# Accumulating DMAs for a spectral sum, and a sixth seven-product down projection, in a two-layer convolution and SwiGLU kernel

## The chip, the cores and the metric

The kernel runs on one core of a Trainium2 chip. The metric is device time in microseconds (us), less is better. TensorE is called PE here (its weight loads PEld), VectorE DVE, ScalarE ACT, GpSimd POOL and SyncE SP, as in the profile. SP, ACT and POOL can each start DMA transfers; "SPq" is SP's DMA queue.

## The reference

Two equal layers work on `x`, 2048 tokens by D = 512 (bf16). A layer is a gated long convolution followed by a SwiGLU block of width F = 1792; both have residuals and layer norms without gain:

```
def layer(x):
    kv = causal_conv4(k, shift_k) * v            # 4 taps on each channel
    y  = irfft(rfft(kv, 2S) * rfft(ssm_k, 2S))[:S] + kv * ssm_D
    x  = x + layernorm(x) * y
    z  = layernorm(x)
    return x + (silu(z @ w_gate) * (z @ w_up)) @ w_down
```

The convolution's result `y` doesn't depend on `x`: it is the same in both layers and computed once.

## The kernel before, in words

**The long convolution.** The sequence is cut into four chunks of 512 tokens. Each chunk of `kv` is turned into a spectrum `X[i]` and each chunk of the filter into a spectrum `G[j]` by matmuls with a DFT matrix. The output chunk k is the inverse transform of `Z[k]`, the sum of the products `X[i]*G[j]` with i+j = k. A spectrum tile is 128 partitions x 4 x 2 x 512 bf16 values, 8 KB in each partition, 1 MB in all; the axis of 2 holds the real and the imaginary part. There are ten products. `product(i, j)` makes one by four DVE operations: two multiplications of 4096 elements (L765, into `t1` and `t2`) and two combinations of 2048 (L769). The first product of a sum is combined right into `Z`; each of the six others into `t1`, and a fifth operation of 4096 elements adds `t1` to `Z` (L773). The inverse begins with `m <- Z` on DVE (L653) for Z[1] to Z[3].

**The SwiGLU blocks.** A unit (layer, c, h) is half h of chunk c in one layer, 256 tokens; there are 16. Gate and up projections go through L423 (and L1171), ACT takes them out of PSUM (L1197, L1198, L1258, L1262), DVE multiplies them (L1204, L1267). Where that was done with tokens on partitions, an SP DMA transposes the result (L1206: `sg <- hr`). Most units do the down projection by 28 matmuls of 512 columns (L1287); ACT copies the two sums out (`dn`, L1332 or L1335) and DVE adds them to `x` (L1339). Five units, those in `STRASSEN`, go through `seven()`: 49 matmuls of 256 columns (L1097) that make seven block products in place of eight. These need sums of activations (`cb`, three DVE operations for each group of tiles, L1076, L1078, L1080), sums of weights made once (`weight_sums`, L1061), and an end of its own (`add_seven`: ACT copies `mt`, L1109, and five DVE operations, L1114 to L1121). The groups hold 4, 4, 4 and 2 tiles.

**Layer norms.** The statistics of two rows of 128 tokens are made on DVE (`ln_stats`: L926 and L927, twice) or on ACT (`ln_stats_act`, L941 to L954), and POOL raises them to the power -1/2 (`rstd`, L912). `ST2` lists the halves whose second layer norm has its statistics on ACT.

**The order of the work.** The program first records all operations with their engine, reads and writes (`add`). The list `ORDER` gives each operation a number, and the operations are issued in this order on their engines; semaphores keep what depends on each other. Buffers come from rings with a fixed count of places (`s8` has 11 of 8 KB; `z` has 3, `jk` one); an operation that takes a place waits for the last reader of what was there.

Of the kernel before, what the change touches and what calls it, by code (L numbers as in the profile page):

```python
# [9 lines left out]
P = 128  # L10
F32 = mybir.dt.float32
# [3 lines left out]
ALU = mybir.AluOpType  # L15
# [6 lines left out]
ST2 = lambda l, c, h: (l, c, h) in {(0, 0, 0), (0, 2, 1), (1, 2, 1)}  # L22
K_ACT = lambda b: b in {2, 3}
PW = 0.7
# [6 lines left out]
STRASSEN={(1,2,1):4,(0,3,0):4,(0,3,1):4,(1,3,0):4,(1,3,1):2}  # L31
# [96 lines left out]
R = 4  # L128
# [222 lines left out]
def kernel(  # L351
# [14 lines left out]
    nc = tc.nc  # L366
# [46 lines left out]
    add = plan.add  # L413
# [326 lines left out]
    def product(i, j, slots=range(4), conv=True):  # L740
# [31 lines left out]
        if not first:  # L772
            dve(8 * D, lambda: nc.vector.tensor_add(out=z.t[:], in0=z.t[:], in1=t1.t[:]), [t1], [z], conv=conv)  # L773
# [832 lines left out]
```

## Time and profile before

| | |
|---|---|
| median of 3 runs | 338.73 us (338.35 to 338.96) |
| span of the profiled execution, first to last instruction | 337.1 us |
| median less that span | 1.63 us |
| granted TensorE clock | 1.000 |
| busy: PE, DVE, ACT, POOL | 332.4, 314.3, 269.4, 36.1 us |
| traffic | 31.08 MB, mean 92 GB/s |

The profiled execution has no time of its own beside its span; the 1.63 us are what the median has over it. The busy time of an engine counts an instruction from its start to its end, and matmuls are pipelined: a row's mean ns of one matmul is longer than the step from one to the next. Steps are therefore read from the chain of waits, where a run of matmuls is one piece with its count.

### The profile page before, as it was taken

Reading aid. Unit: us, or ns where it says so; the run is one execution under the profiler, and the core shown is the slowest. Engines: PE = TensorE matmul, PEld = TensorE weight load, DVE = VectorE, ACT = ScalarE, POOL = GpSimd, SP = SyncE. Lnnn points to the kernel's source line nnn. Section 1 sums busy time; section 2 is a strip of 40 time slices with the busy share of each in tenths; the row PEclk is TensorE's granted clock in tenths of the full one; section 3 lists DMA queues with packets and bytes.
Section 4 is the critical chain, followed back from the end, with each engine's and each line's share of the span. In section 5 each row is a group of like instructions: output and inputs, shape, how many; then the busy total and the mean of one; then the engine's idle time right before and its main releaser. Section 6 shows DMA issues by size and latency. Waiting matters only on the chain.

```text
span 337.1 us, 6249 instructions
## 1 busy us (share of the span) xinstructions
PE 332.4 (99%) x2300; PEld 208.0 (62%) x2300; DVE 314.3 (93%) x566; ACT 269.4 (80%) x550; POOL 36.1 (11%) x48
## 2 busy tenths in 40 slices
PE   9999999999999999999999999999999999999996
PEld 7665865645445564644545474654445787878994
DVE  7799999999999999999999999997898998986995
ACT  6999999999966684989999794989765748476862
POOL 4010100031210100022110200021000000000000
PEclk9999999999999999999999999999999999999999
DMA  7999403632354446253314433320415320203001
GB/s 278 331 281 387 65 3 77 140 93 34 78 94 86 95 88 146 72 80 74 69 33 83 104 81 102 81 53 10 84 33 95 65 65 16 42 8 64 2 33 62
DMA packets 75817, 31.08 MB, mean 92 GB/s; under 512 B 67589, under 2 KB 73610, under 8 KB 75786
## 3 DMA queue, kind: packets, MB, share of 16 engines
q1 hardware_dynamic: 75632, 30.61, 38.3%
q8 instruction: 18, 0.29, 0.4%
q14 instruction: 13, 0.11, 0.1%
q10 hardware_dynamic: 154, 0.07, 0.1%
HBM read 12.33 MB, written 2.10 MB: 43 GB/s over the span
## 4 chain that ended last, share of the span: by engine, by line
PE 85%; DVE 10%; ACT 2%; issue 1%; POOL 0%; POOLq 0%
PE pf L423 48%; PE pd L1287 19%; PE ps L1097 7%; PE ps L423 6%; PE pf L1171 4%; DVE t L755 1%; PE wm L1572 1%; DVE Z L759 1%; DVE bst L926 1%; DVE t L769 1%; ACT jk L950 1%; DVE Z L773 1%; DVE t L765 1%; DVE m L896 1%; DVE z L976 1%
## 5 line engine op out<-in xcount | busy, mean ns | idle before, releaser
L423 PEld LDWEIGHTS <-zT 128*128 128x128 bf16 x496 | 48.5, 98 | 55.1 <-issue 0.2
L423 PE MATMUL pf<-wu_sb,zT 128*128 128x512 bf16 x248 | 61.5, 379 | 0.0
L423 PE MATMUL pf<-wg_sb,zT 128*128 128x512 bf16 x248 | 61.4, 379 | 0.0
L423 PE MATMUL pf<-zT,wg_sb 128*128 128x256 bf16 x400 | 50.7, 273 | 0.3 <-DVE zT L1037 0.3
L1197 ACT ACTIVATE sg<-pf 128x512 bf16<-128x512 f32 x62 | 37.4, 615 | 14.9 <-PE pf L423 10.7
L1287 PE MATMUL pd<-wd_sb,sg 128*128 128x512 bf16 x200 | 48.9, 379 | 0.0
L1198 ACT CAST hr<-pf 128x512 bf16<-128x512 f32 x62 | 36.3, 599 | 12.7 <-PE pf L423 10.9
L423 PEld LDWEIGHTS <-wg_sb 128*128 128x128 bf16 x400 | 38.6, 98 | 8.3 <-issue 0.7
L765 DVE TENSOR_TENSOR t<-X,G 128x4096 bf16<-128x4096 bf16 x18 | 41.0, 2287 | 0.1
L1258 ACT ACTIVATE sg<-pf 128x512 bf16<-128x512 f32 x50 | 29.6, 603 | 7.7 <-PE pf L423 6.3
L423 PE MATMUL pf<-zT,wu_sb 128*128 128x256 bf16 x272 | 34.9, 273 | 0.1
L912 POOL TENSOR_TENSOR rstd<-mv,nhalf 128x2 f32<-128x2 f32 x20 | 18.3, 919 | 147.8 <-DVE mv L927 147.8
L1287 PEld LDWEIGHTS <-sg 128*128 128x128 bf16 x200 | 19.6, 98 | 21.4
L423 PEld LDWEIGHTS <-wu_sb 128*128 128x128 bf16 x272 | 26.5, 98 | 6.6 <-issue 0.4
L1287 PE MATMUL pd<-wd_sb,ht 128*128 128x512 bf16 (+1 forms) x126 | 29.6, 369 | 0.0
L912 POOL TENSOR_TENSOR rstd<-ve,nhalf 128x2 f32<-128x2 f32 x12 | 13.8, 1150 | 119.6 <-ACT ve L954 119.6
L926 DVE BATCH_NORM_STATS2 bst<-xc 128x6 f32<-128x512 bf16 x40 | 26.3, 685 | 0.3
L1262 ACT CAST ht<-pf 128x512 bf16<-128x512 f32 x34 | 20.2, 599 | 1.6 <-PE pf L423 1.5
L1287 PEld LDWEIGHTS <-ht 128*128 128x128 bf16 x126 | 12.3, 98 | 13.4 <-DVE ht L1267 0.4
L532 ACT ACTIVATE X<-ps 128x512 bf16<-128x512 f32 x32 | 18.6, 606 | 2.3 <-PE ps L423 1.6
L1267 DVE TENSOR_TENSOR ht<-ht,sg 128x1024 bf16<-128x1024 bf16 (+1 forms) x33 | 18.3, 556 | 0.7 <-ACT sg L1258 0.4
L1204 DVE TENSOR_TENSOR hr<-hr,sg 128x1024 bf16<-128x1024 bf16 x25 | 17.1, 683 | 1.3 <-ACT sg L1197 0.9
(157 smaller groups left out, 590.9 us busy)
## 6 DMA issues: line engine op xcount, KB each, us to landing
hn<-in_A_ssm_k_dram SPq DMA_DIRECT2D x4, 512.0 KB, 4.0
vt<-in_A_v_dram SPq DMA_DIRECT2D x4, 512.0 KB, 6.0
xc<-in_A_q_dram SPq DMA_DIRECT2D x4, 512.0 KB, 5.3
out_dram<-xc SPq DMA_DIRECT2D x15, 128.0 KB, 1.9
wg_sb<-in_B_w_gate_dram SPq DMA_DIRECT2D x1, 1792.0 KB
wu_sb<-in_B_w_up_dram SPq DMA_DIRECT2D x1, 1792.0 KB, 7.6
wd_sb<-in_B_w_down_dram SPq DMA_DIRECT2D x1, 1280.0 KB, 11.5
sg<-hr SPq DMA_TRANSPOSE x62, 2.4
```

Of the source, the lines that this page charges most:

```text
L423: nc.tensor.matmul(o, lhsT=lhsT, rhs=rhs, start=(n == 0), stop=(n == len(terms) - 1))
L532: add("ACT", act(D), lambda: nc.scalar.activation(out=view(), in_=ps.t[:], func=ACT.Copy, scale=scale), r=[ps], w=[(buf, keys)], conv=conv)
L765: dve(8 * D, lambda t=t, part=part: nc.vector.tensor_mul(out=t.t[:], in0=x.t[:, :, part:part + 1, :].to_broadcast((P, R, 2, D)), in1=g.t[: ...
L912: add("POOL", cost, lambda: nc.gpsimd.tensor_tensor(out=rstd.t[:], in0=var(), in1=nhalf.t[:].to_broadcast((P, n)), op=ALU.pow), r=reads + ...
L926: add("DVE", 0.6, lambda st=st, i=i: nc.vector.bn_stats(out=st.t[:, 0:6], in_=xs[c].t[:, i, :]), r=[(xs[c], (i,))], w=[st])
L1097: nc.tensor.matmul(bank.t[:, half_ * C:(half_ + 1) * C], lhsT=lhsT(i), rhs=rhs(i), start=(first and i == 0 and half_ == 0), stop=(last and ...
L1197: add("ACT", act(D), lambda ps=ps, dst=dst, o=o, which=which: nc.scalar.activation(out=rows(dst, o), in_=ps.t[:], func=ACT.Silu) if which ...
L1198: out=rows(dst, o), in_=ps.t[:], func=ACT.Silu) if which == "g" else nc.scalar.copy(out=rows(dst, o), in_=ps.t[:]),
L1258: add("ACT", act(D), lambda ps=ps, o=o, sg=sg: nc.scalar.activation(out=sg.t[:, o:o + 2, :], in_=ps.t[:], func=ACT.Silu), r=[ps], w=[(sg, ...
L1262: add("ACT", act(D), lambda ps=ps, o=o, ht=ht: nc.scalar.copy(out=ht.t[:, o:o + 2, :], in_=ps.t[:]), r=[ps], w=[(ht, (o // 2,))], due=(uni ...
L1267: dve(n * W, lambda sg=sg, ht=ht: nc.vector.tensor_mul(out=ht.t[:], in0=ht.t[:], in1=sg.t[:]), [sg], [ht], due=(unit, k / pairs, 0.0, "h"))
L1287: nc.tensor.matmul((pds[o] if not cs.start else pds[HP]).t[:, cs], lhsT=ht.tiles(q, o), rhs=wt["d"].t[:, ft, cs], start=(ft == std0 and no ...
```

## The change

1. With `Z_DMA` true for every pair, the L773 addition is replaced by a DMA from POOL with `accum_op=ALU.add`, from `t1` to `Z`, both in SBUF. It is 1 MB each time, for the products (1,0), (0,2), (2,0), (2,1), (0,3) and (3,0). It stands at L778 of the kernel after.
2. Unit (1,2,0) joins `STRASSEN`, so six units go through `seven()`.
3. Unit (1,2,1) leaves `ST2`: the statistics of its second layer norm go from ACT to DVE.
4. The ring `jk` gets a second place, and `fq`, used at the start, moves into ring `z`.
5. A new `ORDER` list.

Lines of the kernel after stand 5 further on up to the rings and 7 further on behind `product` (L912 is L919, L1097 is L1104, L1287 is L1294, L1339 is L1346).

```
-ST2 = lambda l, c, h: (l, c, h) in {(0, 0, 0), (0, 2, 1), (1, 2, 1)}
+ST2 = lambda l, c, h: (l, c, h) in {(0, 0, 0), (0, 2, 1)}
+Z_DMA = lambda i, j: True
-STRASSEN={(1,2,1):4,(0,3,0):4,(0,3,1):4,(1,3,0):4,(1,3,1):2}
+STRASSEN={(1,2,0):4,(1,2,1):4,(0,3,0):4,(0,3,1):4,(1,3,0):4,(1,3,1):2}
-    plan = Plan({..., "n": 2, "jk": 1, ...
+    plan = Plan({..., "n": 2, "jk": 2, ...
-    m4, fq = whole("m4", [P, R], F32), whole("fq", [P, P], F32)
+    m4, fq = whole("m4", [P, R], F32), new("z", "fq", [P, P], F32)
...
-        if not first:
+        if not first and Z_DMA(i, j):
+            add("POOL", 1.3, lambda: nc.gpsimd.dma_start(out=z.t[:], in_=t1.t[:], accum_op=ALU.add, max_dma_last_dim=4096), r=[t1], w=[z], lat=7.0, conv=conv)
+        elif not first:
             dve(8 * D, lambda: nc.vector.tensor_add(out=z.t[:], in0=z.t[:], in1=t1.t[:]), [t1], [z], conv=conv)
```

**Where the additions stood.** DVE's order before, at the last product of the sum for output chunk 2 (`Z_1614` is Z[2], `t1_1857` this product, `m_2029` the first step of its inverse transform):

```order
L769 TENSOR_TENSOR t1_1857<-t1_1857,t2_1792 128x4x512
L1267 TENSOR_TENSOR ht_1970<-ht_1970,sg_1993 128x512 [waits Activation_49]
L773 TENSOR_TENSOR Z_1614<-Z_1614,t1_1857 128x4096 [waits DVE_49]
L653 TENSOR_TENSOR m_2029<-Z_1614 128x2048 [waits DVE_49]
L946 SCALAR_TENSOR_TENSOR nm_2034<-sm_2026,mv_1570 128x2 [waits Activation_49]
```

The inverse follows right behind the addition. DVE's order after, at the same product (`Z_1570` is Z[2], `t1_1820` the product), from its last combination on. `DMASW2` is the transfer's semaphore.

```order
L774 TENSOR_TENSOR t1_1820<-t1_1820,t2_1822 128x4x512
L1068 TENSOR_TENSOR wsb_1918<-wd_sb_391 128x1792
L1211 TENSOR_TENSOR hr_1807<-hr_1807,sg_1814 128x1024 [waits DMAHW5_49,DMAHW4_49,Activation_49]
L934 BN_AGGR mv_1923<-bst_85 128x2 [waits DVE_49]
L983 TENSOR_SCALAR n_1925<-xc_1789,nm_1796,rstd_1868 128x512 [waits Pool_49]
L983 TENSOR_SCALAR n_1925<-xc_1789,nm_1796,rstd_1868 128x512
L1211 TENSOR_TENSOR hr_1902<-hr_1902,sg_1909 128x1024 [waits Activation_49]
L983 TENSOR_SCALAR n_1998<-xc_837,nm_1876,rstd_1900 128x512 [waits Pool_49]
L983 TENSOR_SCALAR n_1998<-xc_837,nm_1876,rstd_1900 128x512
```

The list goes on without a gap:

```order
L1005 TENSOR_TENSOR n_1998<-n_1998,Yk_1325 128x1024 [waits DVE_49]
L1006 TENSOR_TENSOR xc_837<-xc_837,n_1998 128x1024 [waits DVE_49]
L933 BN_STATS bst_85<-xc_837 128x6 [waits DVE_49]
L934 BN_AGGR mv_2004<-bst_85 128x2 [waits DVE_49]
L933 BN_STATS bst_85<-xc_837 128x6
L934 BN_AGGR mv_2004<-bst_85 128x2 [waits DVE_49]
L1274 TENSOR_TENSOR ht_1937<-ht_1937,sg_1981 128x1024 [waits DMAHW2_49,DMAHW1_49,Activation_49]
L933 BN_STATS bst_85<-xc_1789 128x6
L934 BN_AGGR mv_1923<-bst_85 128x2 [waits DVE_49]
L969 SCALAR_TENSOR_TENSOR nmr_2014<-mv_2004,rstd_2012 128x2 [waits Pool_49]
L1274 TENSOR_TENSOR ht_1985<-ht_1985,sg_1996 128x512 [waits Activation_49]
L658 TENSOR_TENSOR m_2056<-Z_1570 128x2048 [waits DMASW2_49]
```

Nineteen other instructions now stand between the last combination and the inverse, and the inverse waits for the transfer.

POOL's order after, around the second and third transfer:

```order
L919 TENSOR_TENSOR rstd_1585<-mv_1535,nhalf_95 128x2 [waits DVE_49,Pool_49]
L778 DMA Z_1570<-t1_1637 128x2x2048 [waits DMAHW2_49,DMASW0_49,DMAHW3_49,DVE_49,DMAHW6_49,PE_49,Activation_49]
L919 TENSOR_TENSOR rstd_1868<-ve_1850,nhalf_95 128x2 [waits Activation_49,Pool_49]
L778 DMA Z_1570<-t1_1820 128x2x2048 [waits DMASW1_49,DVE_49]
L919 TENSOR_TENSOR rstd_1900<-ve_1898,nhalf_95 128x2 [waits Activation_49,Pool_49]
```

Before, only `rstd` rows stood here. A transfer into `Z` waits for the transfer into the same `Z` ahead of it (`DMASW1`), and the `rstd` behind it waits on POOL until it has been issued.

PE's order at the first down matmuls of unit (1,2,0), before:

```order
L423 MATMUL pf_3045<-wu_sb_306,zT_2926 128x512
L1287 LDWEIGHTS sg_2951 [waits DMAHW0_49]
L1287 MATMUL pd_3053<-wd_sb_308,sg_2951 128x512
L1287 LDWEIGHTS sg_2951
L1287 MATMUL pd_3053<-wd_sb_308,sg_2951 128x512
```

and after:

```order
L428 MATMUL pf_3064<-wu_sb_389,zT_2939 128x512
L1104 LDWEIGHTS cb_3070 [waits DVE_49]
L1104 MATMUL ps7_3072<-wsa_1703,cb_3070 128x256
L1104 LDWEIGHTS cb_3070
L1104 MATMUL ps7_3072<-wsa_1703,cb_3070 128x256
L428 LDWEIGHTS zT_2939
```

The down matmuls now read sums made by DVE (`cb`) and sums of weights (`wsa`), have half the columns, and stand in smaller pieces between the gate and up matmuls.

More of the change, by code (lines that the diff above doesn't have):

```diff
@@ L397, in span @@
         return slice(rows[0], rows[-1] + 1, rows[1] - rows[0])
-    plan = Plan({"h": 1, "k": 1, "v": 1, "hs": 1, "dg": 1, "x": 2, "y": 2, "s8":11, "n": 2, "jk": 1, "dn": 1, "ks": 2, "z": 3, "zT":3,
+    plan = Plan({"h": 1, "k": 1, "v": 1, "hs": 1, "dg": 1, "x": 2, "y": 2, "s8":11, "n": 2, "jk": 2, "dn": 1, "ks": 2, "z": 3, "zT":3,
                  "ht":7, "st": 4, "bn": BN_SLOTS, "mv": 9, "ve": 8, "rs": 6, "pf": 4, "pc": 2, "pd": 2, **RINGS})
```

144 rows, old and new, of the table ORDER are left out of this document.

## The prediction

> **What bounds the kernel now.** First the page's counts and its chain that ended last.
>
> ```profile
> span 337.1 us, 6249 instructions
> PE 332.4 (99%) x2300; PEld 208.0 (62%) x2300; DVE 314.3 (93%) x566; ACT 269.4 (80%) x550; POOL 36.1 (11%) x48
> PE 85%; DVE 10%; ACT 2%; issue 1%; POOL 0%; POOLq 0%
> ```
>
> TensorE is on the path for 85% of the span, DVE for 10%. Where that tenth lies is told by busy times of each engine in stretches of the program (columns: stretch, length, PE, PEld, DVE, ACT, POOL, granted clock, DMA share, GB/s).
>
> ```profile
> 0.00:33.00 33.00, 31.73 (x295) 21.76 (x295) 28.74 (x74) 29.03 (x59) 5.97 (x18) 1.00 1.00 319
> 33.00:230.00 197.00, 196.91 (x1118) 109.33 (x1119) 193.74 (x278) 169.48 (x351) 23.75 (x21) 1.00 0.38 80
> 230.00:260.00 30.00, 30.00 (x161) 15.37 (x159) 25.91 (x38) 21.91 (x47) 2.87 (x4) 1.00 0.29 58
> 260.00:331.00 71.00, 70.84 (x711) 59.75 (x709) 63.48 (x173) 48.14 (x95) 3.47 (x5) 1.00 0.17 37
> 331.00:337.10 6.10, 2.95 (x22) 1.83 (x19) 2.38 (x5) 0.84 (x3) 0.00 (x0) 1.00 0.26 86
> ```
>
> From 33 to 331 us TensorE is idle for 0.09 + 0.00 + 0.16 = 0.25 us. The idle time is in the first 33 us, where the transfers are at 319 GB/s, and in the tail. So after 33 us the kernel takes as long as its matmul stream. DVE is nearly full itself (193.74 of 197.00), but it only paces the stream if it falls behind. What TensorE waits for, in total, times and longest:
>
> ```profile
> PE ptz L1034 <- DVE z L976: 0.3, 1, 0.3
> PE pf L423 <- DVE zT L1037: 0.3, 1, 0.3
> PEld L1287 <- DVE ht L1267: 0.4, 1, 0.4
> PEld L1097 <- DVE cb L1076: 0.3, 1, 0.3
> PEld L1097 <- DMA sg<-hr: 0.2, 1, 0.2
> PEld L423 <- DMA zT<-z: 0.2, 1, 0.2
> ```
>
> Each of these happens once. There is no repeated wait for DVE that 13.7 us less of additions could end. I conclude that DVE time taken away is worth almost nothing by itself; what counts is what it pays for, the shorter matmul stream of unit (1,2,0).
>
> **The matmul stream.** Runs of matmuls in the chain (start, us, count):
>
> ```profile
> 222.47 4.32 PE pd L1287 x20
> 326.54 4.69 PE ps L1097 x43
> 33.09 4.53 PE pf L423 x40
> ```
>
> A 512-column step is 4.32/20 = 0.216 us, a 256-column one 4.69/43 = 0.109 us. Unit (1,2,0) loses 28 x 0.216 = 6.05 us and gains 49 x 0.109 = 5.34 us. That is **-0.71 us**, wholly on the path. The third row is the first SwiGLU run, at 33.09 us. By the new order the matmuls ahead of it take one 512-column step more, so if the run starts at the same time, work that stood behind is done in an idle place: **-0.22 us**.
>
> **DVE.** The groups by shape (busy us, mean ns):
>
> ```profile
> L773 DVE TENSOR_TENSOR Z<-Z,t 128x4096 bf16<-128x4096 bf16 x6 | 13.7, 2287 | 0.0
> L926 DVE BATCH_NORM_STATS2 bst<-xc 128x6 f32<-128x512 bf16 x40 | 26.3, 685 | 0.3
> L927 DVE BATCH_NORM_AGGREGATE mv<-bst 128x2 f32<-128x9 f32 x40 | 6.3, 182 | 0.2
> L1339 DVE TENSOR_TENSOR xc<-xc,dn 128x1024 bf16<-128x1024 bf16 x11 | 7.5, 684 | 0.0
> L1076 DVE TENSOR_TENSOR cb<-ht 128x512 bf16<-128x512 bf16 x8 | 3.3, 422 | 0.1
> L1080 DVE TENSOR_TENSOR cb<-ht 128x256 bf16<-128x256 bf16 x8 | 2.3, 286 | 0.0
> L1114 DVE TENSOR_TENSOR xc<-xc,mt 128x1024 bf16<-128x1024 bf16 x5 | 3.4, 688 | 1.3 <-ACT mt L1109 1.3
> ```
>
> Removed: six additions, 13.72. The sixth unit adds, for each of its three groups of four tiles, two sums at 0.42 and one at 0.286, and for the last group three of at most 0.286: 4.2. Its end adds 0.69 + 4 x 0.42 = 2.4 and takes away the `dn` addition, 0.68. The statistics of unit (1,2,1) come to DVE: 2 x 0.685 + 2 x 0.182 = 1.7. Net -13.7 + 4.2 + 2.4 - 0.7 + 1.7 = **-6.1 us of DVE**. ACT loses those statistics and gains two copies; at 80% busy it is not near the path. I put all this at nothing: the cover is the matmul stream itself, which is without gaps from 33 to 331 us.
>
> **The accumulating transfers.** No row of before shows one; all its DMAs come from SP and ACT, and none adds. The nearest rows (KB each, median us to landing):
>
> ```profile
> hn<-in_A_ssm_k_dram SPq DMA_DIRECT2D x4, 512.0 KB, 4.0
> vt<-in_A_v_dram SPq DMA_DIRECT2D x4, 512.0 KB, 6.0
> out_dram<-xc SPq DMA_DIRECT2D x1, 64.0 KB, 1.6
> ```
>
> From below: from the last row to the first, 448 KB cost 2.4 us, 5.4 ns a KB, so 1024 KB take 4.0 + 512 x 0.0054 = 6.7 us; at the 387 GB/s of the page's busiest slice, 2.7 + 1.6 = 4.3. From above: `vt` carried on at its own slope, (6.0 - 1.6)/448 = 9.8 ns, lands 1 MB at 11.0; if reading the target counts as a second megabyte, the `hn` slope gives 1.6 + 1984 x 0.0054 = 12.3. I take 7 us, nearest to `hn`, and keep 4.3 and 12.3 as ends.
>
> What an accumulate costs is what its reader waits for beyond its cover, the DVE work listed between the last combination and the reader. DVE's timeline shows how work adds up (start, us):
>
> ```profile
> 67.81 2.35 DVE L769 TENSOR_TENSOR t<-t,t 128x2048 bf16<-128x2048 bf16 x2
> 70.08 2.29 DVE L765 TENSOR_TENSOR t<-X,G 128x4096 bf16<-128x4096 bf16 x1
> 72.28 2.29 DVE L773 TENSOR_TENSOR Z<-Z,t 128x4096 bf16<-128x4096 bf16 x1
> 74.48 0.69 DVE L1339 TENSOR_TENSOR xc<-xc,dn 128x1024 bf16<-128x1024 bf16 x1
> ```
>
> Starts are 2.20 apart where one lasts 2.29, so each instruction gives 0.085 to the next. In the shortest cover (Z[2]'s last product, shown above) 19 instructions stand: 1.09 of weight sums, 4 of 1024 elements at 0.69, one of 512 at 0.42, 4 scalings at 0.41, 3 statistics at 0.685, 3 aggregates at 0.182 and one small at 0.15, in all 9.5 - 19 x 0.085 = **7.9 us**. The same count gives 9.7 for the first transfer, 9.4 for the second, 9.0 for the last and about 25 for the fourth; the fifth is waited for only by the sixth. At 7 us none waits: **0**.
>
> The POOL queue holds `rstd` behind each transfer. Behind the third, `rstd_1900` is needed 3.45 - 6 x 0.085 = 2.9 us after the last combination. An `rstd` takes 0.69 us alone, but beside DVE work on two inputs it took longer:
>
> ```profile
> 57.93 0.69 POOL L912 TENSOR_TENSOR rstd<-ve,nhalf 128x2 f32<-128x2 f32 x1 [10.73 <-ACT ve L954]
> 72.85 2.86 POOL L912 TENSOR_TENSOR rstd<-ve,nhalf 128x2 f32<-128x2 f32 x1 [7.29 <-ACT ve L954]
> ```
>
> The second started within the L773 addition above and ended 1.1 us after it. The issue of a transfer on POOL isn't in the trace; between nothing and 2.86 us, with the 0.69 behind it, it is 0.7 to 3.6 against 2.9. I take 0.69 for the issue, as for the free `rstd`, so no wait.
>
> [...]
>
> **Sum.** The profiled execution: 337.1 - 0.71 - 0.22 = 336.2 us; its span is 1.63 us below the median shown, so **337.8 us**, -0.93 or -0.27%.
>
> **Rivals.**
>
> *A, slower: the accumulates land late.* [...] It decides from 7.9 us on. If POOL is held as at 72.85, by 2.17 us, landing is 9.2: waits of 1.3 and 0.2, half of that on the path, 338.6 (chance 0.07). [...] At 11 us the waits are 1.3 + 1.6 + 3.1 + 2.0 = 8.0 us; DVE has 6.1 us less to do, but spread over the whole stretch, so I let half through: 337.8 + 4.0 = 341.8. At 12.3 it is 13 us, half 6.6: 344.4. Against it: the slower `vt` ran beside other loads at the start, and traffic is 80 GB/s where the accumulates stand.
>
> *B, slower: the megabytes delay the transposes.* Beside the later 512 KB load of `vt` (issued at 61.7 us) the transposes of `sg` took up to 3.3 us, not 2.4:
>
> ```profile
> L495 SPq DMA_DIRECT2D vt<-in_A_v_dram x1: 578/578/578, 61.7 to 61.7; - x1
> DMA to landing us min/median/max: 2.4/2.6/3.3
> ```
>
> Two waits of TensorE above are for transposes already, so some have no time to spare. If two of the six transfers catch such a one, 2 x 0.9: 339.6; if all do, 343.2.
>
> *C, no change: the sixth unit's saving is lost.* DVE must deliver `cb` ahead of the 256-column matmuls. One wait there was 0.3 us; three more, in four groups, eat the 0.9: 338.7. Lost likewise if the transfer's issue holds `rstd_1900` for its 0.7 us.
>
> *D, faster by more.* DVE is no longer full, so the idle 0.25 us goes and up to half of the first 33 us' 33.00 - 31.73 = 1.27: 336.9.
>
> **Chances.** Forecast (337.4 to 338.2) 0.47; A 0.18, 0.07 of it mild; B 0.13; C 0.14; D 0.08. A measurement of this kernel can tell about 0.2% (0.68 us) from no change, so faster ends at 338.05 and slower begins at 339.41. Faster: D and most of the forecast, 0.50. Same: C, the rest of the forecast, the mild case of A and part of B, 0.22. Slower: 0.28. The range goes from 336.6, under D, to 342.0, above A at 11 us; A at 12.3, B's end and what I haven't thought of are left out.
>
> **What would show it.** Right: about 0.25 us of idle TensorE between 33 and 331 us, L1104 with 273 matmuls and L1294 with 286, no wait of DVE at L658 or L770 for a transfer, DVE near 308 us busy. A: idle time before `m <- Z` at L658, and accumulates of over 8 us. B: waits of PEld for `sg<-hr` or `zT<-z`, and transposes above 2.4 us. C: PEld waiting for `cb`, or DVE for `rstd`. The prediction is wrong if the start moved: a first SwiGLU run that begins a microsecond later than 33.09 outweighs the saving.

## The result, and the profile after

The changed kernel takes 355.85 us (354.57 to 356.9, 4 runs) against 338.54 us (338.27 to 338.96, 4 runs): ratio 1.051, 95% interval 1.048 to 1.054. It is 17.3 us slower. The forecast was 337.8 us, with 342.0 as the upper end.

The page after, from the same parts as before, with the new queue and the new transfer:

```profile
span 355.1 us, 6289 instructions
PE 335.1 (94%) x2291; PEld 210.2 (59%) x2321; DVE 310.8 (88%) x580; ACT 268.6 (76%) x542; POOL 39.9 (11%) x54
q0 software_dynamic: 1632, 6.29, 10.0%
PE 68%; DMA 11%; DVE 9%; ACT 6%; issue 2%; SPq 2%; POOL 1%; DVEq 0%; ACTq 0%; POOLq 0%
Z<-t POOLq DMA_DIRECT2D x6, 1024.0 KB, 8.4
```

DVE has 310.8 us, 3.5 less, but DMA, which had no share of the chain that ended last, now has 11% of it. The six accumulates land in 8.4 us (median). TensorE's waits (total, times, longest):

```profile
PE pd L1294 <- DMA sg<-hr: 7.8, 4, 4.0
PE ps L428 <- DVE vt L734: 4.6, 1, 4.6
```

The first is a wait for SP's transposes of `sg`. The second is for DVE, but DVE itself stood there waiting for the `kc` transposes. DVE waited only once for an accumulate, at L770, where the next product writes into a ring place that the second transfer was still reading:

```profile
DVE vt L734 <- DMA kc<-ka: 5.0, 1, 5.0
DVE t L770 <- DMA Z<-t: 1.6, 1, 1.6
```

The chain around the second and third accumulate shows the mechanism (start, us, what):

```profile
125.85 8.90 DMA sg<-hr
134.75 0.05 issue
134.79 5.79 PE pd L1294 x20
140.58 3.24 PE pf L428 x15
...
147.65 6.01 DMA sg<-hr
153.67 0.27 issue
153.94 6.17 PE pd L1294 x20
```

A transpose that took 2.4 us took 8.9 and 6.0. It was issued while an accumulate was in flight, and it landed just behind it. (The two transposes had been issued 2.1 and 3.5 us behind the accumulates.) POOL's timeline has the issue of the second accumulate, and the answer on the tile `Z` from 120 to 126 us its time to landing:

```profile
123.71 1.23 POOL L778 DMA_DIRECT2D Z<-t  x1 [15.78 <-ACT sg L1265]
```

```profile
DMA to landing us min/median/max: 10.6/10.6/10.6
```

123.7 + 10.6 = 134.3, against 125.85 + 8.90 = 134.75 for the transpose. Likewise the third accumulate landed at 152.6 and the transpose at 147.65 + 6.01 = 153.7.

Behind such a wait the matmuls are slow as well: 20 steps took 5.79 and 6.17 us, where 20 took 4.32 before. The stretches show the granted clock there (columns as in the prediction; the clock is the last but two):

```profile
130.00:134.80 4.80, 0.76 (x5) 0.15 (x3) 3.16 (x3) 2.49 (x7) 0.71 (x1) 0.92 1.23 173
134.80:138.00 3.20, 3.20 (x9) 1.23 (x10) 3.09 (x2) 0.00 (x0) 0.00 (x0) 0.58 0.68 149
138.00:146.00 8.00, 7.95 (x39) 3.77 (x39) 4.66 (x9) 5.60 (x14) 1.87 (x2) 1.00 0.03 5
154.00:158.00 4.00, 4.00 (x11) 1.45 (x11) 3.56 (x6) 2.39 (x4) 0.00 (x0) 0.57 0.71 194
205.00:209.00 4.00, 3.92 (x11) 1.52 (x12) 3.76 (x9) 2.16 (x4) 0.00 (x0) 0.59 0.50 102
```

After each of the three long waits (4.0, 2.9 and 4.6 us) the granted clock is 0.57 to 0.59 for some 3 to 4 us, then 0.99 to 1.00 again (1.00 from 138 to 146 and from 158 to 170 us, 0.99 from 209 to 220 us). The length of a wait alone doesn't decide it: in the experiments below TensorE's longest wait is 2.0 us in e1 as in e9, and the mean granted clock of the profiled execution is 1.000 in e1 and 0.995 in e9.

**Where the 18 us went** (spans, 355.1 - 337.1): three waits of 4.0 + 2.9 + 4.6 = 11.5 us; slow steps behind them, 1.5 and 1.9 us by the two rows of 20 and some 1.7 at 205 us (4 us at 0.59), together 5. The remaining 1.5 us are short waits such as 0.9 us for `cb` sums, less the shorter stream.

### The profile page after: what moved, and what is told of

Its sections match the earlier page's. It is cut to its first block, busy times and chain, and to the rows that moved or that the text cites. A ratio compares the mean times of both kernels' runs of the same rounds, so it can differ in the third digit from the quotient of the medians.

```text
span 355.1 us, 6289 instructions
## 1 busy us (share of the span) xinstructions
PE 335.1 (94%) x2291; PEld 210.2 (59%) x2321; DVE 310.8 (88%) x580; ACT 268.6 (76%) x542; POOL 39.9 (11%) x54
## 4 chain that ended last, share of the span: by engine, by line
PE 68%; DMA 11%; DVE 9%; ACT 6%; issue 2%; SPq 2%; POOL 1%; DVEq 0%; ACTq 0%; POOLq 0%
PE pf L428 36%; PE pd L1294 17%; DMA sg<-hr 8%; PE ps L1104 7%; PE ps L428 4%; PE pf L1178 3%; DMA kn<-in_A_k_dram 1%; DVE t L760 1%; DMA kc<-ka 1%; SPq L730 1%; ACT jk L957 1%; ACT sg L1204 1%; DVE Z L764 1%; DVE bst L933 1%; ACT hr L1205 1%
## 5 line engine op out<-in xcount | busy, mean ns | idle before, releaser
L1294 PE MATMUL pd<-wd_sb,sg 128*128 128x512 bf16 x169 | 44.7, 402 | 8.1 <-DMA sg<-hr 7.8
L428 PE MATMUL pf<-zT,wg_sb 128*128 128x256 bf16 x400 | 49.4, 273 | 0.0
L770 DVE TENSOR_TENSOR t<-X,G 128x4096 bf16<-128x4096 bf16 x18 | 41.2, 2288 | 1.8 <-DMA Z<-t 1.6
L1265 ACT ACTIVATE sg<-pf 128x512 bf16<-128x512 f32 x50 | 29.3, 609 | 13.6 <-PE pf L428 8.2
L919 POOL TENSOR_TENSOR rstd<-mv,nhalf 128x2 f32<-128x2 f32 x21 | 19.0, 904 | 152.8 <-DVE mv L934 143.9
L1294 PEld LDWEIGHTS <-sg 128*128 128x128 bf16 x176 | 17.4, 101 | 29.6 <-DMA sg<-hr 9.6
L1294 PE MATMUL pd<-wd_sb,ht 128*128 128x512 bf16 (+1 forms) x119 | 28.9, 381 | 0.2
L933 DVE BATCH_NORM_STATS2 bst<-xc 128x6 f32<-128x512 bf16 x42 | 28.0, 683 | 0.4
L1104 PEld LDWEIGHTS <-cb 128*128 128x128 bf16 x195 | 18.8, 98 | 4.4 <-DVE cb L1087 1.9
L1294 PEld LDWEIGHTS <-ht 128*128 128x128 bf16 x122 | 12.4, 102 | 14.5 <-issue 2.7
L1116 ACT CAST mt<-ps 128x512 bf16<-128x512 f32 (+1 forms) x24 | 12.6, 538 | 8.1 <-PE ps L1104 7.8
```

The costliest lines, as they stand in the source:

```text
L428: nc.tensor.matmul(o, lhsT=lhsT, rhs=rhs, start=(n == 0), stop=(n == len(terms) - 1))
L770: dve(8 * D, lambda t=t, part=part: nc.vector.tensor_mul(out=t.t[:], in0=x.t[:, :, part:part + 1, :].to_broadcast((P, R, 2, D)), in1=g.t[: ...
L919: add("POOL", cost, lambda: nc.gpsimd.tensor_tensor(out=rstd.t[:], in0=var(), in1=nhalf.t[:].to_broadcast((P, n)), op=ALU.pow), r=reads + ...
L933: add("DVE", 0.6, lambda st=st, i=i: nc.vector.bn_stats(out=st.t[:, 0:6], in_=xs[c].t[:, i, :]), r=[(xs[c], (i,))], w=[st])
L1104: nc.tensor.matmul(bank.t[:, half_ * C:(half_ + 1) * C], lhsT=lhsT(i), rhs=rhs(i), start=(first and i == 0 and half_ == 0), stop=(last and ...
L1265: add("ACT", act(D), lambda ps=ps, o=o, sg=sg: nc.scalar.activation(out=sg.t[:, o:o + 2, :], in_=ps.t[:], func=ACT.Silu), r=[ps], w=[(sg, ...
```

## The experiments

Theory **T**: a 1 MB accumulate holds back the transposes that SP issues while it is in flight, TensorE waits for these, and the lower clock behind the waits adds to it. Rivals: **O**, the new order list or the sixth unit cost the time; **P**, it is the adding, not the megabyte; a fixed price of each accumulate, wherever it stands; and on the mechanism, **W**, a transpose waits until the whole transfer is done. Each experiment is the changed kernel with one edit, unless said otherwise.

| | us (range) | ratio to before, 95% |
|---|---|---|
| e1: additions on DVE again | 351.65 (350.25 to 353.31) | 1.039 (1.035 to 1.043) |
| e2: an eighth accumulated | 339.04 (338.83 to 342.44) | 1.0028 (1.0008 to 1.0048) |
| e3: 512-byte pieces | 372.18 (371.76 to 374.06) | 1.101 (1.098 to 1.104) |
| e4: plain copies | 342.93 (342.06 to 344.38) | 1.014 (1.010 to 1.017) |
| e5: before, with unread accumulates | 381.21 (380.58 to 382.38) | 1.125 (1.121 to 1.128) |
| e6: the fourth accumulate later | 359.02 (357.8 to 359.74) | 1.060 (1.056 to 1.063) |
| e8: e6, and two additions on DVE | 352.69 (351.51 to 353.13) | 1.041 (1.038 to 1.044) |
| e9: DMAs only where none met | 346.35 (345.52 to 346.82) | 1.023 (1.021 to 1.024) |
| e10: DMAs only where they met | 360.44 (359.56 to 360.7) | 1.065 (1.063 to 1.066) |

### e2: an eighth of the traffic

```
-nc.gpsimd.dma_start(out=z.t[:], in_=t1.t[:], accum_op=ALU.add, max_dma_last_dim=4096)
+nc.gpsimd.dma_start(out=z.t[:, 0, 0, :], in_=t1.t[:, 0, 0, :], accum_op=ALU.add, max_dma_last_dim=4096)
```

> Each accumulating DMA moves one eighth (512 of 4096 values a partition, 128 KB); the other seven eighths of the six products are not added, so the result lacks them. Everything else as in the changed kernel. Theory T: the transfer is over in about 3 us, no transpose lands after more than 5 us, and the time is that of the forecast, 337 to 339 us. Rival O: over 350 us. [...]

Measured 339.04 us: theory T, and not O. List, sixth unit, waits and POOL issues are all there; only seven eighths of the bytes are gone, and with them 16.8 us. TensorE's two waits, now:

```profile
PE pd L1294 <- DMA sg<-hr: 0.6, 2, 0.3
...
PE ps L428 <- DVE vt L734: 0.3, 1, 0.3
```

The accumulates of line 778 (the issue on POOL in ns, then the landing):

```profile
L778 POOL DMA_DIRECT2D Z<-t x6: 901/901/1067, 71.0 to 228.3; - x6
...
DMA to landing us min/median/max: 2.7/2.8/5.0
```

It also measures the rest of the change, apart from the traffic: the ratio is 1.0028 where the forecast was 0.9973. So the sixth unit and the new list together gained nothing. The stretches show TensorE idle for 1.08 us from 33 to 332 us, where it was 0.25 before:

```profile
33.00:120.00 87.00, 86.36 (x494) 47.74 (x492) 85.11 (x125) 79.49 (x162) 9.24 (x11) 1.00 0.41 86
120.00:215.00 95.00, 94.75 (x526) 51.20 (x525) 92.80 (x135) 80.98 (x167) 15.86 (x14) 1.00 0.41 87
215.00:260.00 45.00, 45.00 (x286) 27.24 (x284) 40.54 (x84) 29.66 (x62) 6.53 (x7) 1.00 0.32 59
260.00:300.00 40.00, 39.81 (x377) 32.43 (x375) 34.65 (x96) 25.01 (x49) 1.78 (x3) 1.00 0.20 41
```

More than half of it is ahead of 120 us, and what TensorE waits for there, from 108 to 116 us, is `sg` again, with no accumulate near (one ended at 74 us, the next starts at 123): in the new list these transposes land in 2.4 to 2.5 us, as before, but come too late for TensorE.

```profile
PEld L1294 <- DMA sg<-hr: 1.6, 2, 0.8
```

The 0.8 us more of idle time eat the 0.71 us by which the stream should be shorter.

### e4: the same megabyte without adding

```
-accum_op=ALU.add, max_dma_last_dim=4096
+max_dma_last_dim=4096
```

> The same 1 MB transfers from POOL, but as plain copies of t1 over Z, so the sums hold the last product only. Theory P (reading, adding and writing back makes the transfer long): landing falls from 8.4 to 4.5 to 6 us, the transposes wait for that much less, and the time is 342 to 350. Rival (the 1 MB itself is what counts, adding is free): landing 8 to 9 us and about 355 us.

Measured 342.93 us, at the lower end of P. The copies land in 5.1 us, and their packets take half the time of the accumulates' for the same count and bytes (4.9% of a 340.3 us span, 10.0% of 355.1 with adding):

```profile
q0 software_dynamic: 1632, 6.29, 4.9%
...
Z<-t POOLq DMA_DIRECT2D x6, 1024.0 KB, 5.1
```

TensorE's waits:

```profile
PE pd L1294 <- DMA sg<-hr: 2.2, 3, 1.5
PE ps L428 <- DVE vt L734: 1.2, 1, 1.2
```

The same two waits stand in the same places, at 1.5 and 1.2 us where the accumulates had 4.0 and 4.6. Behind these the granted clock stays at 1.00; the chain behind the first:

```profile
125.47 6.33 DMA sg<-hr
131.80 0.05 issue
131.84 4.49 PE pd L1294 x20
```

20 matmuls in 4.49 us, against 5.79 behind the longer wait. So both count: the megabyte makes the transposes late at all, the adding makes it last long enough to hurt.

### e3: smaller pieces

```
-accum_op=ALU.add, max_dma_last_dim=4096
+accum_op=ALU.add, max_dma_last_dim=512
```

> The same six accumulates cut into pieces of 512 bytes instead of 4096. [...] Rival W (a transpose waits until the whole transfer is done, whatever its packets): landing 6 to 9 us as before, about 355 us.

Measured 372.18 us, and as a way out it is a miss: the accumulates grow to 13.0 us (median). DVE now waits 6.5 us for a ring place that one of them still reads, and an inverse step waits 2.6 us for its `Z`. The page's row of the transfer, and DVE's waits:

```profile
Z<-t POOLq DMA_DIRECT2D x6, 1024.0 KB, 13.0
```

```profile
DVE t L770 <- DMA Z<-t: 6.5, 1, 6.5
...
DVE m L658 <- DMA Z<-t: 2.6, 1, 2.6
```

On the mechanism it says a little. The third accumulate was issued at 147.3 us and landed after 13.6, at 160.9; the first `sg` transpose beside it was issued at 148.7 and landed after 7.2, at 155.9, five microseconds ahead of the accumulate. In the changed kernel, with 4096-byte pieces, no transpose issued more than 1 us behind an accumulate landed ahead of it, as far as the trace has their landings. So W doesn't hold whatever the pieces. The counts of pieces moved (queue, pieces, MB, share; q0 is the accumulate's queue, q1 SP's) are of the changed kernel from 147 to 150 us, with transposes issued at 145.46 and 147.65, and of e3 from 156 to 159 us:

```profile
q0 software_dynamic: 139, 0.57, 108.4%
...
q0 software_dynamic: 589, 0.30, 95.1%
q1 hardware_dynamic: 528, 0.13, 47.5%
```

In the first stretch nothing of a transpose moves, as W has it; in the second, with pieces of 512 bytes, the two go nearly one for one (589 and 528). No run shows why the transposes start so late beside pieces of 4096 bytes; that stays open.

### e1: the additions back on DVE

```
-Z_DMA = lambda i, j: True
+Z_DMA = lambda i, j: False
```

> The new order list, the sixth unit and all else of the change stay; only the six accumulating DMAs are DVE additions again, at the same places. Theory T (the 1 MB transfers hold back the SP transposes, and TensorE waits for these): transposes land in 2.4 us again (longest under 4.5), no wait of TensorE for sg or kc of over 1 us, clock back at 1.000. DVE has 13.7 - 6.1 = 7.6 us more than before, in stretches where it was 98% busy, so 338 to 345 us. Rival O (the new list or the sixth unit cost the time): still over 350 us, with the waits of 3 to 5 us in place.

Transposes are quick again (`sg` 2.5 us, longest 4.1) and the clock of the profiled execution is 1.000, as T has it, but the time is 351.65 us, well above its 345, and in the range of O. O's waits of 3 to 5 us aren't there, though; none is above 2.0 us.

```profile
PE pd L1294 <- DMA sg<-hr: 4.0, 5, 1.7
PE pf L428 <- ACT hr L1205: 2.9, 2, 1.7
PE ps L428 <- DVE vt L734: 2.0, 1, 2.0
PE pf L428 <- ACT sg L1204: 1.6, 1, 1.6
```

Six additions of 2.2 us that the list made no room for cost 351.65 - 339.04 = 12.6 us, 2.1 each: here TensorE pays for nearly every microsecond of DVE. I had compared totals (7.6 us more than before), but in a list without slack an operation is paid where it stands. This run alone would leave O open; e2 closes it.

### e9 and e10: the same number of DMAs, in other places

Beside three accumulates, (1,0), (0,3) and (3,0), no transpose whose landing the trace has took over 3 us; the others, (0,2), (2,0) and (2,1), met transposes of 7.7 to 8.9 us. Each kernel keeps three.

```
-Z_DMA = lambda i, j: True
+Z_DMA = lambda i, j: (i, j) in {(1, 0), (0, 3), (3, 0)}      # e9
+Z_DMA = lambda i, j: (i, j) in {(0, 2), (2, 0), (2, 1)}      # e10
```

> In the changed kernel only the three accumulates beside which no transpose was held long (products (1,0), (0,3), (3,0)) are DMAs; the other three are DVE additions. Theory T (what costs is the meeting with transposes): 339.0 us of the kernel with an eighth accumulated, and what those three additions cost when all were on DVE, 1.4 + 1.8 + 0.4 + 2.2 = 5.8: about 345, 343 to 347 us, no transpose over 5 us. Rival (a fixed price of each accumulate, 16.8/6 = 2.8 us): 339.0 + 8.4 + 5.8 = 353 us.

> The other way round: the three accumulates that met transposes (products (0,2), (2,0), (2,1)) are DMAs, the other three DVE additions. Theory T: all of the changed kernel's loss stays, and the three additions come to it, 1.75 + 1.85 + 1.78 = 5.4 us in the kernel with all on DVE: 355.85 + 5.4, about 361, 358 to 364 us, waits of TensorE of 4, 3 and 5 us for sg and kc. Rival (a fixed price of each accumulate): 353 us, as the kernel with the other three.

Measured 346.35 and 360.44 us: T's 345 and 361, not the one price of 353 for both. TensorE's waits in e10:

```profile
PE pd L1294 <- DMA sg<-hr: 10.2, 5, 5.1
PE ps L428 <- DVE vt L734: 4.4, 1, 4.4
```

In e9 the longest landing of `sg` is 4.3 us, as before the change, and in e10 9.9. Three accumulates cost next to nothing (1.5 us above T's sum; the two runs in which the granted clock stayed at 1.000 took 345.5 and 346.0 us), three others of the same size all of the loss.

### e6 and e8: an accumulate moved, and moved wrongly

In e6 the fourth accumulate stands behind the last `kc` transpose in the list; e8 has the second and third as DVE additions besides.

```
+LATER = [((2, 1), 'kc', -1)]
...
+        for pair, name, nth in LATER:
+            o = next(o for o in seq if getattr(o, "behind", None) == pair)
+            seq.remove(o)
+            at = [k for k, x in enumerate(seq) if x.eng == "SP" and any(b.name == name for b in x.bufs)][nth]
+            seq.insert(at + 1, o)
```

> The changed kernel with the fourth accumulate (product (2,1)) issued behind the last kc transpose instead of ahead of them, some 13 us later, where SP has no transpose for some 10 us; its reader is far off. All else stays. Theory T: the wait of TensorE for vt and kc at 200 us (4.7 us) goes, and with it the slow stretch behind it (1.7 us), so 349 to 351 us. Rival O, or a fixed price of each accumulate: about 355.8 us.

> As the fourth moved, and the two accumulates that met sg transposes at 125 and 146 us (products (0,2) and (2,0)) are DVE additions again. Theory T: what remains is the 339.0 us of the kernel with an eighth accumulated and what these two additions cost in that list, 1.4 and 1.8 us of TensorE waiting when all six were on DVE: 341 to 344 us, transposes at most 5 us. Rival: a fixed price of each accumulate, (355.85 - 339.04)/6 = 2.8 us: four of them and the two additions, 353 us.

Measured 359.02 and 352.69 us; both expectations failed. The list only orders POOL's own instructions: the accumulate passed one `rstd` and went at 197.54 us, not some 13 us later. The last `kc` transpose, behind which it stands in the list, was issued at 199.66 us, still behind it, and so was an `sg` transpose at 198.39 us, which I had left out of account. The two took 7.8 and 8.4 us. POOL's timeline of e6, ACT's, and TensorE's wait:

```profile
197.54 1.22 POOL L784 DMA_DIRECT2D Z<-t  x1
```

```profile
207.52 1.57 ACT L543 ACTIVATE X<-ps 128x512 bf16<-128x512 f32 x3 [8.79 <-DMA kc<-ka]
```

```profile
PE pf L434 <- ACT X L543: 6.8, 1, 6.8
```

The wait at 200 us grew from 4.6 to 6.8 us, now by way of ACT, which stood waiting for that `kc` transpose until it landed at 207.4 us. That e8 comes out at the 353 of a fixed price has this cause: the wait of the fourth accumulate was still in it. These two runs don't tell T from the rivals; e9 and e10, made in their place, do. In e8 the same wait is 6.9 us; with it and its slow clock gone one would be near the 341 to 344 expected, but that is arithmetic and wasn't run.

### e5: the kernel before, with accumulates that nobody reads

Six accumulates from `t1` into the dead `t2`, each behind a product's last combination; no engine's order is changed.

```
+            add("POOL", 1.3, lambda: nc.gpsimd.dma_start(out=t2.t[:], in_=t1.t[:], accum_op=ALU.add, max_dma_last_dim=4096), r=[t1], w=[t2], lat=7.0, conv=conv)
```

> The kernel before with all its DVE additions, its list and its five units, and beside them six accumulating DMAs of 1 MB from POOL, each started where the change starts its own (right behind a product's last combination), from t1 into the dead t2, which nobody reads; every engine's own order is as before. Two of DVE's inverse steps may wait because their buffer was t2. Theory T (megabyte transfers hold back transposes, wherever the program): transposes issued beside them land in 5 to 9 us, TensorE waits several us for sg, zT or vt, and the time is 345 to 365 us. Rival O (the new list or the sixth unit make the transposes late): transposes stay at 2.4 us, at most 4.3 as before, and TensorE waits for none of them over 1 us.

Measured 381.21 us, above the 345 to 365 expected. Here five units and the old list lose 43 us to the accumulates and to the waits for their buffers: O isn't needed for a loss. `sg` transposes land after up to 7.8 us, `kc` transposes after up to 8.2. The size is no price of the transposes, though: two DVE operations waited for the buffer of `t2`, 16 us, and part of TensorE's waits comes from those. DVE's waits, and one of TensorE's that is for a transpose:

```profile
DVE wu L1143 <- DMA t<-t: 8.5, 1, 8.5
DVE m L660 <- DMA t<-t: 7.5, 1, 7.5
```

```profile
PE pd L1297 <- DMA sg<-hr: 4.8, 1, 4.8
```

No run was faster than the kernel before. The best, e2, isn't a version (it leaves additions out) and marks what this list would reach if the transfers were nearly free: 0.5 us above before.

## Why the prediction was wrong

- **The bound.** Right: TensorE was without gaps from 33 us, so DVE's relief could be worth nothing by itself. The same row meant that every late transfer is paid in full, and I drew that only as a rival.
- **The step that failed: "What an accumulate costs is what its reader waits for beyond its cover".** By its own measure it was nearly right: with a landing of 8.4 and not 7 us no reader of a `Z` waited, and the one wait for an accumulate was the 1.6 us at L770. The cost came from transfers that have nothing to do with the accumulate. They were in rival B, with the right mechanism and a wrong size: I took 0.9 us for a late transpose, from a 512 KB load beside which they took 3.3 us. The changed kernel shows up to 8.9 us, a delay of 6.5: a transpose issued early in an accumulate landed just behind it (at 134.75 us and 134.3). The chance of B, 0.13, and its 339.6 us followed from that size; even its upper end, 343.2, is 12.7 below the result.
- **What I had in hand.** TensorE was already waiting 0.2 us for two transposes before. With a transpose at 2.4 us and the accumulate bound at 4.3 to 12.3 us, the end for a transpose that waits for it to finish is 12.3 and not 3.3. I bounded the reader's wait from both sides, but not the neighbour's.
- **The clock** was in no step. The three waits of 2.9 to 4.6 us cost 5 us more in slow steps.
- **The landing.** 8.1 to 10.6 us against 7, within the ends given. A plain copy of 1 MB takes 4.5 us at the least in e4, an accumulate of the same size 8.1 here: adding nearly doubles it.
- **POOL.** The issue takes 1.22 us, not 0.69; no long wait for `rstd` came from it: the one of 3.0 us at L983 is in e1 too, without any DMA there (2.7 us).
- **Sixth unit, -0.71 and -0.22 us.** The counts are as forecast, and e2's first SwiGLU run starts 0.3 us earlier, but 0.8 us of new waits took the gain: rival C in its size, mostly by late `sg` transposes (TensorE's wait for `cb` in e2 is 0.2 us).
- **DVE.** 310.8 us against the 308 forecast. The durations of its instructions add up to 5.9 us less, near the 6.1 of the sum; the busy time, which counts an overlap once, fell by 3.5.
- **Slips in the working.** The list of the shortest cover names four operations of 1024 elements and three aggregates, where the order shown has five and four; its 9.5 and 7.9 us are those of all 19. The chances don't add up to the verdicts: slower can be at most 0.11 of A and the 0.13 of B, 0.24 and not 0.28. Neither decides the miss.

## What to carry to other kernels

A transfer costs not only what its reader waits for: look up which small transfers are issued while it is in flight, how much time they have to spare, and take as the worst case that they land when it does (here at 134.75 us beside an accumulate that landed at 134.3). Where the engine that bounds the kernel has no gaps, a long wait can be paid twice, the second time by the clock: here the waits of 4.0, 2.9 and 4.6 us were, the 1.5 and 1.2 us of e4 were not. An order list without slack can't be judged by sums of busy time: an operation more or less is paid at its place.

## What the hardware showed that was not expected

- An accumulate of 1 MB from SBUF to SBUF takes 8.1 us with no transpose issued beside it, a plain copy 4.5 us at the least (e4); an accumulate of 128 KB 2.7 us (e2). From the two accumulates, (8.1 - 2.7)/896 KB is 6.0 ns a KB. The 10.6 us of the second accumulate come with a 512 KB load (`xc`) that SP issued 0.3 us behind it; up to 127 us the load's pieces alone were moving.
- The pieces matter (e3's rows of line 778; the changed kernel's had 1222 ns and 8.4 us in the middle):

```profile
L778 POOL DMA_DIRECT2D Z<-t x6: 2113/2125/2275, 70.9 to 256.4; - x6
...
DMA to landing us min/median/max: 12.0/13.0/15.6
```

  That is, with 512 bytes in place of 4096 the accumulates take 13.0 us in place of 8.4 (median), and the issue on POOL 2.1 us in place of 1.22.
- SP is held up as well: its issue of a transpose takes 1.2 us, and beside an accumulate of the changed kernel it took up to 3.1 us.
